# Other figures for DMA transfers in a kernel's own instruction planner

## The chip, the cores and the metric

The kernel runs on one core of one Trainium2 chip. The metric is device time in microseconds, the median of the runs. Work is spread over the engines PE (TensorE, matmuls), DVE (VectorE), ACT (ScalarE), POOL (GpSimd) and SP (SyncE). In this kernel SP does nothing but issue transfers (DMAs), all on one hardware queue.

## The reference

Inputs are x (8 batches, 4224 positions, 192 channels), generator weights (8, 4224, 8 heads, 7 taps), w1 (192 x 768) and w2 (768 x 192); the last two are float64. First a causal dynamic convolution, then an FFT mixing block with a two-layer network:

```python
w = softmax(weight_gen, axis=-1)                 # 7 taps per position and head
x_unf = windows of 7 positions of x_pad          # zeros ahead of the first
x = einsum('bshk,bskhg->bshg', w, x_unf)         # 8 heads of 24 channels
mixed = real(fft(fft(x, axis=1), axis=2))
u = x + mixed
un = (u - mean(u)) / sqrt(var(u) + 1e-6)         # over the 192 channels
out = u + maximum(un @ w_ch1, 0) @ w_ch2
```

## The kernel before, in words

A batch's 4224 positions lie as 128 partitions by 33 rows. Each batch passes through these stages:

- `conv(b)`: loads the generator weights (tile `w`) and x (`x_sb`, in pieces of 192 to 864 KB), makes the softmax on DVE and ACT (`wm`), multiplies rows by taps on DVE (`pr`) and sums them on POOL (`u`). In the first batch some sums run on PE (`pa`). Rows are folded on POOL (`sm`), multiplied by a DFT table on PE (`pg`), put together on DVE (`gt`) and stored to scratch DRAM `g_d`.
- `transform(b)`: loads scratch back as `g` in another layout, multiplies by tables on PE (`pp`) and copies to `pq` on ACT.
- `mix(b, g)`: PE matmuls (`eo`), with sums into `u` on DVE.
- `norm(b, g)`: for one of nine groups of four rows, statistics on ACT (`junk`, `st`, `rs`), normalized rows `un`, split into two float16 parts (`hl`), transposed by DMA into `ht`. For most groups a further DMA copies 64 rows of `ht` to the other partitions as `hd`.
- `mlp(n)`: first products into `ph` on PE, with w1 and the activations as float16 pairs. A part of them uses half of the array's rows: matmuls from `ht` and from `hd` run side by side, alternating. ACT and DVE turn `ph` into the hidden units `hh`; second products go to `po`; DVE adds `po` to `u`, and SP stores `u` to `out`.

None of this is issued as it is written. The functions record operations on a `Tape`. `plan` puts them in order, and `emit` issues each engine's instructions in exactly that order (all at line 408, which is why the profile's rows have that line).

`plan` finds for each operation what it must wait for, then walks all operations as a simulation with one clock for each engine. At each step it takes the earliest moment at which something can start, and of the operations of one engine that can start then, the one of lowest rank. `cost` gives two times for an operation: how long the engine is taken, and how long until the result is there. For transfers it adds a third, the time on the wire. The forward walk keeps one queue for all transfers (`wire`); the backward walk has none. Nine forward rounds at most: the first in the order as written, then up to eight times a backward walk, whose result says how late each operation may start, and two forward walks ranked by that (one of them mixed with the last start times). The plan whose modelled end comes first is kept.

Three rules of the walk matter here. A tile's buffer must be free before its first operation. A group of half-array matmuls is a *visit*: it opens with its first matmul, which reads `ht`, and while it is open PE takes matmuls of that visit alone as long as any of them is waiting. And a transfer occupies SP for 400 ns (1450 for a transpose) in the model, whatever its size.

For a transfer, "run" is the number of elements that lie together on both sides, and the wire time is the number of such runs times a cost per run.

Of the kernel before, what the change touches and what calls it, by code (L numbers as in the profile page):

```python
# [48 lines left out]
POOL_TAPS = {(0, 0): (5, 6), (0, 1): (5, 6), (0, 3): (6,), (1, 0): range(7), (1, 1): range(7)}  # L49
DVE_ADDS = {(1, c): 1 for c in range(2, NC)}  # L50
HOLD3 = 3
WIRE = 0.7

F32_GROUPS = 7
ACT_ROWS = 4
# [121 lines left out]
def together(ap):  # L177

    run = 1
    for step, n in reversed(ap.ap[1:]):  # L180
        if n > 1 and step != run:
            break
        run *= n
    return run
# [7 lines left out]
def cost(op):  # L192

    lane, reads, writes = op.lane, op.reads, op.writes
    count = lambda ap: int(np.prod([n for _, n in ap.ap[1:]]))
    out = writes[0]
    n = max(map(count, reads + writes))
    if lane == "pe":
        n = count(out)
        t = 2 * max(112 if 64 < n <= DH else 56, 0.855 * n) if reads[0].dtype == F32 else max(55.8, 0.417 * n + 2.4)  # L200
        if op.visit:
            return t / 2, t + 178
        return t, t + 178
    if lane == "sp":
        if op.kw.get("transpose"):
            return 1450, 2000 + 1.2 * n, 1.09 * n
        size, run = BYTES[out.dtype], min(together(ap) for ap in reads + writes)
        return 400, 2000 + WIRE * count(out) * size, out.ap[0][1] * count(out) / run * (0.5 + 0.0023 * run * size)
    if lane == "dve":
        t = 150 + (6.27 if op.call == "reciprocal" else 1.042) * n + (60 if len(reads) == 3 and n < 512 else 0)  # L210
        return t - 83, t
    if lane == "pool":
        t = 183 + (1.92 if out.dtype == F16 else 2.13) * n
        return t - 45, t
    t = 190 + (0.833 if out.ap[-1][0] == 1 else 1.666) * n + 90 * (len(reads) - 1)
    return (t + 100, t + 90) if len(writes) > 1 else (t - 95, t)


def plan(tape):
# [29 lines left out]
    for lo, hi, first in tape.holds:  # L249
        for op in ops[lo:min(hi, len(ops))]:  # L250
            if op.lane == first.lane:
                op.needs.setdefault(first.index, False)

    costs = [cost(op) for op in ops]
    before, after = [op.needs for op in ops], [{} for _ in ops]
    for k, needs in enumerate(before):
# [14 lines left out]
    def walk(rank, rows, back=False):  # L271

        to, left = (before, after) if back else (after, before)
        left, ready, span = [len(n) for n in left], [0.0] * len(ops), [None] * len(ops)
        uses = {name: len(set(users[name])) for name in row_of}
        ends, placed, heads = defaultdict(float), {}, {row: 0 for row in rows}
        spare = {row: [(-1e3, i) for i in range(homes[names[0]].bufs)] for row, names in rows.items()}
        free, waiting = {lane: 0.0 for lane in HOP}, {lane: set() for lane in HOP}
        order, table, wire = [], None, 0.0
        half, stays = None, defaultdict(int)  # L280
        taken, wanted = defaultdict(int), {}
        for v in visits:
            stays[v] += 1
        door = set() if back else {span[0] for span in enters.values()}
        for k, n in enumerate(left):
            if n == 0:
                waiting[lanes[k]].add(k)

        def claim(name):

            kind = homes[name].use
            if kind == "fft" and taken["fft"] >= FFT:
                return BANKS
            group = family[name]
            return sum(n for g, n in wanted.items() if g != group)

        def opens(k):

            t = ready[k]
            for name in tiles[k]:  # L300
                if name not in placed:
                    row = row_of[name]
                    if back or row != SHARED:
                        while rows[row][heads[row]] in placed:
                            heads[row] += 1
                        if rows[row][heads[row]] != name:
                            return None
                    if not spare[row] or (row == SHARED and not back and len(spare[row]) <= claim(name)):
                        return None
                    t = max(t, min(spare[row])[0] + HOP[lanes[k]] + (ROOM if row == SHARED else 0))  # L310
            if k in door:
                if len(spare[SHARED]) < 3:
                    return None
                t = max(t, sorted(spare[SHARED])[2][0] + HOP["pe"] + ROOM)
            return t

        for _ in ops:
            at = [(max(free[lane], t), rank[k], k) for lane, ks in waiting.items()
                  for t, k in ((opens(k), k) for k in ks) if t is not None]
            if not at:  # L320
                return None
            if half and stays[half]:
                at = [a for a in at if lanes[a[2]] != "pe" or visits[a[2]] == half] or at
            now = min(at)[0]
            lane = next(lane for lane in HOP if any(t == now and lanes[k] == lane for t, _, k in at))
            k = min((r, k) for t, r, k in at if t == now and lanes[k] == lane)[1]
            if kinds[k] and kinds[k] != table:
                now, table = now + 1283, kinds[k]
            if lane == "pe":
                if visits[k] != half:  # L330
                    now, half = now + VISIT, visits[k]
                stays[half] -= 1
            waiting[lane].remove(k)
            order.append((now, k))
            busy, done, *load = costs[k]
            free[lane], end = now + busy, now + done
            if load and not back:
                wire = max(wire, now + 1000) + load[0]
                end = max(end, wire + 1000)
            span[k] = now, end  # L340
            for name in tiles[k]:
                row = row_of[name]
                if name not in placed:
                    spot = min(spare[row])
                    placed[name] = spot[1]
                    if row == SHARED:
                        taken[homes[name].use] += 1
                        group = family[name]
                        if group in groups:
                            if group not in wanted:  # L350
                                wanted[group] = 6
                            wanted[group] -= 1
                            if not wanted[group]:
                                del wanted[group]
                    spare[row].remove(spot)
                uses[name] -= 1
                ends[name] = max(ends[name], end)
                if not uses[name]:
                    spare[row].append((ends[name], placed[name]))
                    if row == SHARED:  # L360
                        taken[homes[name].use] -= 1
            for j, sync in to[k].items():
                loose = lanes[j] == lane and (lane == "pe" or not sync)
                ready[j] = max(ready[j], now if loose else end + HOP[lane if back else lanes[j]] + (SLACK if lanes[j] != lane else 0))
                left[j] -= 1
                if left[j] == 0:
                    waiting[lanes[j]].add(j)
        return max(end for _, end in span), span, order, placed

    best = now = walk(list(range(len(ops))), rows)  # L370
    for _ in range(TURNED):
        last = {name: max(now[1][k][1] for k in users[name]) for name in row_of}
        turned = walk([-end for _, end in now[1]], {row: sorted(names, key=lambda name: -last[name]) for row, names in rows.items()}, True)
        if turned is None:
            break
        late = [turned[0] - end for _, end in turned[1]]
        now = min((w for w in (walk([part * t + (1 - part) * s for t, (s, _) in zip(late, now[1])], rows) for part in (1.0, 0.8)) if w),
                  key=lambda w: w[0], default=None)
        if now is None:
            break  # L380
        best = min(best, now, key=lambda w: w[0])
# [935 lines left out]
```

## Time and profile before

| | |
|---|---|
| time, median of 3 runs | 1091.94 us (1090.03 to 1092.83) |
| the profiled execution | 1091.01 us |
| its span, first to last instruction | 1089.2 us |
| mean granted TensorE clock | 0.995 |
| PE busy | 1064.2 us, 98% |
| DVE, POOL, ACT busy | 952.3, 871.4, 789.3 us |
| DMA | 130.20 MB, the one queue busy 44.7% of 16 engines |

How to read the rows: a row of waits says who waited for whom, the sum in us, how often, and the longest. A row of the timeline has start, length, engine, line, operation, out<-in, shape and count, and in brackets the idle time before it with what ended it; rows of SP are issues and not transfers. A row of the chain of waits (the work that ended last, followed back) has start and length; where it names a DMA, the length runs from issue until the waiting engine was released. In rows by window each engine has its busy time and, in brackets, its instructions.

### The profile page before, as it was taken

What the parts mean: (1) busy time and instruction counts of PE and PEld (TensorE: products, weight loads), DVE (VectorE), ACT (ScalarE), POOL (GpSimd) and SP (SyncE); (2) the same over time, 40 slices, a digit from 0 to 9 for tenths busy, and PEclk for the clock granted to TensorE, in tenths of its full rate; (3) what the DMA queues carried; (4) which work ended last, traced back from release to release, by engine and by line L of the source; (5) the groups of instructions that cost most, each with busy time, mean ns of one, the idle gap of its engine ahead of it and who ended that gap; (6) DMA issues with size and microseconds to landing.
All of it is one profiled execution on the core that took longest, in us unless ns stands there. A gap on an engine that the chain in (4) does not pass through costs nothing.

```text
span 1089.2 us, 23832 instructions
## 1 busy us (share of the span) xinstructions
PE 1064.2 (98%) x8596; PEld 807.7 (74%) x8596; DVE 952.3 (87%) x1737; ACT 789.3 (72%) x2385; POOL 871.4 (80%) x759
## 2 busy tenths in 40 slices
PE   7899999999999999999999999999999999999998
PEld 5467788886767867687778777687768877786777
DVE  7999998889999998999999999999999998345443
ACT  4575877568874887678886787778786888589842
POOL 4979899799989999799979999799969999102200
PEclk8999999999999999999999999999999999999999
DMA  8554145615484346714564356614554333612311
GB/s 296 158 147 109 31 110 173 157 40 143 101 210 108 83 118 189 153 57 140 129 183 111 98 115 205 146 58 129 147 142 112 79 68 76 147 51 72 90 54 48
DMA packets 166125, 130.20 MB, mean 120 GB/s; under 512 B 119533, under 2 KB 142710, under 8 KB 166006
## 3 DMA queue, kind: packets, MB, share of 16 engines
q1 hardware_dynamic: 166006, 128.67, 44.7%
q8 instruction: 68, 1.11, 0.4%
q14 instruction: 51, 0.42, 0.1%
HBM read 60.38 MB, written 39.43 MB: 92 GB/s over the span
## 4 chain that ended last, share of the span: by engine, by line
PE 54%; DVE 16%; POOL 15%; issue 7%; ACT 4%; DMA 3%; SPq 0%; DVEq 0%; POOLq 0%; ACTq 0%
PE po L408 22%; PE ph L408 22%; POOL u L408 12%; DVE pr L408 5%; PE eo L408 3%; PE pp L408 3%; DVE u L408 3%; DVE wp L408 2%; PE pg L408 2%; PE pa L408 2%; DVE hh L408 2%; ACT junk L408 1%; POOL hl L408 1%; POOL sm L408 1%; DMA g<-g_d 1%
## 5 line engine op out<-in xcount | busy, mean ns | idle before, releaser
L408 POOL TENSOR_TENSOR u<-u,pr 128x768 f32<-128x768 f32 (+1 forms) x396 | 655.9, 1677 | 18.8 <-DVE pr L408 6.9
L408 PE MATMUL po<-w2h,hh 128*128 128x192 f16 x2832 | 423.1, 247 | 1.8 <-DVE hh L408 1.3
L408 PEld LDWEIGHTS <-hh 128*128 128x128 f16 x4248 | 366.1, 99 | 44.2 <-DVE hh L408 1.9
L408 PE MATMUL ph<-ht,w1h 128*128 128x512 f16 (+1 forms) x1296 | 389.7, 362 | 2.1 <-DMA ht<-hl 1.7
L408 DVE TENSOR_TENSOR pr<-x_sb,wp 128x768 f32<-128x768 f32 (+1 forms) x409 | 349.4, 879 | 21.6 <-POOL u L408 17.0
L408 PE MATMUL po<-w2l,hh 128*128 128x192 f16 x1416 | 347.8, 246 | 0.0
L408 ACT ACTIVATE hh<-ph 128x512 f16<-128x512 f32 (+2 forms) x400 | 220.4, 590 | 113.3 <-PE ph L408 82.1
L408 DVE SCALAR_TENSOR_TENSOR hh<-ph,hh 128x512 f16<-128x512 f32 (+1 forms) x358 | 234.1, 680 | 60.1 <-ACT hh L408 59.9
L408 PE MATMUL ph<-ht,w1l 128*128 128x512 f16 (+2 forms) x696 | 230.2, 358 | 0.0
L408 PEld LDWEIGHTS <-w1h 128*128 128x128 f16 x1296 | 127.4, 99 | 109.7 <-issue 25.9
L408 POOL TENSOR_TENSOR hl<-un,hl 128x512 f16<-128x512 f32 (+1 forms) x138 | 116.9, 860 | 73.6 <-issue 40.7
L408 ACT ACTIVATE un<-u,rs 128x192 f32<-128x192 f32 x264 | 126.6, 538 | 23.5 <-POOL rs L408 16.5
L408 ACT ACTIVATE junk<-u,st 128x192 f16<-128x192 f32 x252 | 114.2, 453 | 4.7
L408 ACT ACTIVATE junk<-u 128x192 f16<-128x192 f32 x252 | 91.1, 362 | 28.4 <-DVE u L408 25.1
L408 PEld LDWEIGHTS <-w1l 128*128 128x128 f16 (+1 forms) x864 | 64.1, 97 | 53.5 <-issue 18.0
L408 DVE SCALAR_TENSOR_TENSOR u<-po,isc,u 128x384 f32<-128x384 f32 (+1 forms) x122 | 73.1, 599 | 22.2 <-PE po L408 22.0
L408 PE MATMUL eo<-cs_sb,pq 97*128 97x97 f32 x544 | 88.2, 273 | 0.3 <-ACT pq L408 0.2
L408 PEld LDWEIGHTS eo<-cs_sb,pq 97*128 97x128 f32 x544 | 79.2, 191 | 8.1 <-DVE hh L408 1.2
L408 POOL TENSOR_TENSOR sm<-u 128x382 f32<-128x382 f32 (+1 forms) x128 | 75.7, 608 | 5.8 <-ACT u L408 5.8
L408 ACT COPY pq<-pp 97x204 f32<-97x204 f32 (+3 forms) x176 | 47.2, 314 | 37.4 <-PE pp L408 33.8
L408 PE MATMUL po<-w2f,hh 128*128 128x192 f32 x336 | 74.3, 327 | 0.0
L408 DVE TENSOR_TENSOR u<-u,eo 128x380 f32<-128x380 f32 (+3 forms) x160 | 71.5, 491 | 0.6
(92 smaller groups left out, 1168.8 us busy)
## 6 DMA issues: line engine op xcount, KB each, us to landing
out_dram<-u SPq DMA_DIRECT2D x64, 384.0 KB
x_sb<-in_x_dram SPq DMA_DIRECT2D x48, 384.0 KB
x_sb<-in_x_dram SPq DMA_DIRECT2D x8, 864.0 KB
g<-g_d SPq DMA_DIRECT2D x40, 162.0 KB
g_d<-gt SPq DMA_DIRECT2D x32, 195.0 KB
g_d<-gt SPq DMA_DIRECT2D x32, 189.0 KB
g<-g_d SPq DMA_DIRECT2D x40, 144.0 KB
w<-in_weight_gen_dram SPq DMA_DIRECT2D x6, 924.0 KB
```

The source lines that it names most:

```text
L408: ins = getattr(getattr(nc, op.engine), op.call)(*map(found, op.args), **{n: found(a) for n, a in op.kw.items()}).ins
```

## The change

Only the planner's figures for transfers change; `WIRE` is used in `cost` alone.

```diff
-WIRE = 0.7
+WIRE = 0.5
...
     if lane == "sp":
         if op.kw.get("transpose"):
-            return 1450, 2000 + 1.2 * n, 1.09 * n
+            return 1450, 2000 + 1.2 * n, 1.15 * n
         size, run = BYTES[out.dtype], min(together(ap) for ap in reads + writes)
-        return 400, 2000 + WIRE * count(out) * size, out.ap[0][1] * count(out) / run * (0.5 + 0.0023 * run * size)
+        return 400, 1750 + WIRE * count(out) * size, out.ap[0][1] * count(out) / run * (1.35 + 0.0035 * run * size)
...
             if load and not back:
-                wire = max(wire, now + 1000) + load[0]
-                end = max(end, wire + 1000)
+                wire = max(wire, now + 440) + load[0]
+                end = max(end, wire + 1200)
```

All times are in ns. `count(out)` is the number of elements in one partition, `size` the bytes of one, `out.ap[0][1]` the number of partitions, and `n` the largest count of a transpose's operands (1536 for a full group). The instructions and the transfers are the same before and after; their order on each engine and the buffers that tiles get can differ.

## The prediction

> **What bounds the kernel now.** I read the page's first two parts, then PE's waits, split at 120 us because the picture changes there.
>
> ```profile
> span 1089.2 us, 23832 instructions
> PE 1064.2 (98%) x8596; PEld 807.7 (74%) x8596; DVE 952.3 (87%) x1737; ACT 789.3 (72%) x2385; POOL 871.4 (80%) x759
> PE   7899999999999999999999999999999999999998
> ```
>
> PE is busy 98% of the span, in nearly every slice. The change adds and removes no instruction, so PE's 1064.2 us stay, and what an order of work can win is in the 25.0 us left. Of those, PE waited as follows, first up to 120 us, then from 120 us on.
>
> ```profile
> PE pa L408 <- DVE pr L408: 5.8, 5, 3.6
> PE pg L408 <- POOL sm L408: 2.6, 4, 1.2
> ```
>
> ```profile
> PE ph L408 <- DMA hd<-ht: 2.7, 1, 2.7
> PE ph L408 <- DMA ht<-hl: 1.7, 2, 0.9
> PE po L408 <- DVE hh L408: 1.3, 1, 1.3
> PE ph L408 <- DVE hh L408: 0.5, 1, 0.5
> PE pp L408 <- DMA g<-g_d: 0.7, 1, 0.7
> ```
>
> Up to 120 us PE waits for products and folds, not for transfers. Later transfers are most of it: 2.7 + 1.7 + 0.7 = 5.1 us. Only there can better figures for transfers pay at once. The largest wait also costs clock; the windows show PE's busy time first, then the other engines, then the granted clock before the last two columns.
>
> ```profile
> 384.00:388.00 4.00, 1.37 (x6) 0.39 (x4) 4.00 (x8) 3.48 (x14) 4.00 (x4) 1.00 0.48 174
> 388.00:392.00 4.00, 3.93 (x21) 2.46 (x22) 3.96 (x8) 2.41 (x8) 4.00 (x6) 0.60 0.19 38
> 392.00:396.00 4.00, 4.00 (x31) 2.96 (x29) 2.00 (x5) 2.27 (x7) 4.00 (x4) 0.97 0.39 76
> ```
>
> After the idle 2.70 us the clock is 0.60 for 4 us and 0.97 for 4 more: 4 x 0.40 + 4 x 0.03 = 1.72 us of matmul time. This one wait is thus worth 2.70 + 1.72 = 4.42 us, more than all other transfer waits of PE after 120 us (2.4 us).
>
> **The change, part by part.** Four edits, all in the planner's account of a transfer. Their direct cost on the chip is nothing: what changes is the order on each engine, and which buffer a tile gets.
>
> First, the latency and the bytes (2000 + 0.7 per byte of a partition becomes 1750 + 0.5). For 3072 bytes, a 384 KB load, a store, or a load of g, a lone transfer goes from 4.15 to 3.29 us; the hd copy (1024 bytes) from 2.72 to 2.26 us. Second, queue time (0.5 + 0.0023 per byte of a run becomes 1.35 + 0.0035, times the runs): a 384 KB load takes the queue for 1.55 instead of 0.97 us, an 864 KB load 3.27 instead of 2.10, a hd copy (256 runs of 256 bytes) 0.57 instead of 0.28. Third, the fixed parts around the queue go from 1000 + 1000 to 440 + 1200 ns. Fourth, a transpose holds the queue 1.77 instead of 1.67 us; its own latency is left alone.
>
> So a lone transfer is planned earlier, and one behind others later. The backward walk, which gives the urgencies, has no queue, so it sees only the shorter latencies. Which set is nearer to the chip? The chain of waits has transfers with their true time from issue to release (start, length, what):
>
> ```profile
> 0.74 2.88 DMA w<-in_weight_gen_dram
> ...
> 197.93 3.75 DMA g_d<-gt
> ...
> 202.10 2.93 DMA g<-g_d
> ...
> 340.94 2.65 DMA g<-g_d
> ...
> 684.23 2.88 DMA hd<-ht
> ...
> 808.14 2.87 DMA g_d<-gt
> ...
> 812.30 4.51 DMA g<-g_d
> ```
>
> By the old figures: 3.57, 4.15, 4.15, 4.15, 2.78, 4.15, 4.15; by the new: 2.99, 3.29, 3.29, 3.29, 3.30, 3.29, 3.7 (the last behind three loads of g). The old miss by 0.79 us on average, the new by 0.46. The transfer that PE stood still for, with what SP issued just ahead of it and the sizes of those:
>
> ```profile
> 379.70 0.85 SPq L408 DMA_DIRECT2D out_dram<-u  x1
> 380.61 1.16 SPq L408 DMA_DIRECT2D x_sb<-in_x_dram  x2
> 381.87 0.62 SPq L408 DMA_DIRECT2D hd<-ht  x1
> ```
>
> ```profile
> x_sb<-in_x_dram SPq DMA_DIRECT2D x1, 864.0 KB
> x_sb<-in_x_dram SPq DMA_DIRECT2D x1, 384.0 KB
> out_dram<-u SPq DMA_DIRECT2D x1, 96.0 KB
> ```
>
> ```profile
> 381.87 6.16 DMA hd<-ht
> ```
>
> ```profile
> 384.98 0.39 PE L408 MATMUL ph<-ht,w1l 64*128 64x512 f16 x1
> 388.07 0.39 PE L408 MATMUL ph<-hd,w1l 64*128 64x512 f16 x1 [2.70 <-DMA hd<-ht]
> ```
>
> Replayed with the true issue times, taking the 864 KB first. Old: the store ends on the queue at 380.99, the big load at 381.61 + 2.10 = 383.71, the next at 384.68, the copy at 384.96, seen at 385.96. New: the store at 380.66, then 381.05 + 3.27 = 384.32, 385.87, 386.44, seen at 387.64. In truth 388.02. The old figures hide 2.1 us of this delay from the planner, the new ones 0.4. An order that looked almost free (PE reaches the visit at 384.98, about 1 us early by the old account) now looks 2.7 us dear. I therefore take it that the plan chosen from the walks avoids it: -4.42 us. Both ends: 0 if the order there stays, and -4.42 - 2.4 = -6.8 if the ht and g waits go as well. I take -4.42 because a transpose's own latency is not touched, so nothing points at the ht waits.
>
> [...]
>
> **What is late next.** Where the plan moves the copy ahead of the x loads, these land 0.57 us later by the new account. Who waits for them is the next batch's products on DVE and the sums on POOL. Both are full at that place (4.00 of 4 us above), so they have a backlog to work through, and this costs 0 while it lasts. If that cover is gone, it costs the 0.57 us, once for each batch: 4.0 us over 7 batches. Where the plan lets PE do other products first, the copy's hidden units on ACT and DVE move later by the same 2.7 us, and the second products of that group behind them; PE has the previous group's second products as cover.
>
> **The sum.** The profiled execution took 1091.01 us, 1.8 us more than its span of 1089.2. 1091.01 - 4.42 = 1086.6 us. The median of the three runs, 1091.94, is 0.93 us higher, so for a median I add that: 1087.5 us.
>
> **The rivals.** (a) *Nothing of weight changes.* The walk is greedy: it lets PE enter a visit of half products when ht is there, whatever it knows of hd, and then stays. Knowing the true landing does not by itself stop it, and about 1 us of this wait was accepted already. The stall then stays or comes up elsewhere at the same price: 1091.9 us, with 1088.7 to 1095.2 as what can't be told from no change (0.3% of 1091.94 is 3.3 us). For it: the edits move planned times by about 1 us where PE's backlog covers most. Against it: 497 transfers move, and the walk sorts exact times, so one changed landing can reorder all that follows it.
>
> (b) *The other side: more visits entered before their copy lands.* The list of issues counts the copies:
>
> ```profile
> hd<-ht SPq DMA_DIRECT2D x56, 64.0 KB
> ```
>
> PE stalls at one of the 56. A lone copy is planned 0.46 us sooner, so visits are entered sooner; a copy that falls behind one 864 KB load then costs 4.42 us as priced above. With the stall kept and one more: 1091.9 + 4.4 = 1096.4; two more: 1100.8. It decides from the first net extra stall, since 4.4 is over 3.3. For it: the chosen entry does not look at hd. Against: wherever something big is queued ahead the new figures are later, not sooner.
>
> (c) *The queue times are too long where the queue is really full.* Over the first 20 us, in 40 slices of 0.5 us:
>
> ```profile
> GB/s 0 0 0 40 139 394 377 419 430 151 34 194 373 221 387 359 387 334 450 392 395 430 410 418 365 410 416 406 406 399 399 412 393 399 393 395 407 390 395 398
> DMA packets 2453, 6.56 MB, mean 328 GB/s; under 512 B 253, under 2 KB 765, under 8 KB 2453
> ```
>
> The chip moves about 400 GB/s from 10 us on. The old figure for a 384 KB load is 393216 / 0.97 = 406 GB/s, the new 254. So at the start the old figures are right, and the new plan thinks the later x, table and weight loads arrive up to some 9 us later than they do (6.56 MB at 254 instead of 400 GB/s). If it puts the second half of the softmax on DVE behind products that are not needed yet, the taps after it come later by that block:
>
> ```profile
> 12.34 1.50 DVE L408 TENSOR_REDUCE wm<-w 128x184 f32<-128x1288 f32 x1
> ...
> 14.00 1.49 DVE L408 TENSOR_TENSOR w<-w,wm 128x1288 f32<-128x1288 f32 x1
> ...
> 18.91 1.50 DVE L408 TENSOR_REDUCE wm<-w 128x184 f32<-128x1288 f32 x1
> ...
> 21.70 1.31 DVE L408 RECIPROCAL wm<-wm 128x184 f32<-128x184 f32 x1
> ```
>
> That is 5.8 us, giving 1091.9 + 5.8 = 1097.7, and it decides from 3.3 us, a little more than half of the block. Against it: between 13 and 60 us no row of the engines' waits names a transfer, so the loads have slack, and by the new account this piece (644 KB) is planned for 12.9 us, close to where it is used.
> [...] The trace is on both sides: 400 GB/s here, and a copy at 388.02 that only the longer queue time explains.
>
> **How the numbers follow.** The stall gone, nothing like it new: 0.42, at 1087.5, own range 1083 to 1088.7. It includes 1085.1, where the ht and g waits go too. (a) 0.25. (b) 0.20, since a new order of 23832 instructions finds new places as easily as it loses old ones. (c) 0.10. The rest, 0.03, is a start that gets worse in another way. So faster 0.42, within 0.3% 0.25, slower 0.33. The range of 8 in 10 takes in one and two extra stalls above, and below the 1085.1 and some of PE's 8.4 us of waits up to 120 us: 1081 to 1101.
>
> **What would show it.** PE's wait for hd gone or under 1 us and the granted clock at 1.00 between 360 and 420 us; PE busy still about 1064 us; the 384 and 864 KB loads no longer just ahead of a copy that a visit waits for. PE's first product of the hidden layer is this row:
>
> ```profile
> 104.01 0.38 PE L408 MATMUL ph<-ht,w1h 128*128 128x512 f16 x1 [0.31 <-DVE bn L408]
> ```
>
> Wrong, if there are waits of PE for hd at two or more places (b), or if that first product comes over 3 us later than 104 us (c). If PE's waits for DVE hh grow instead, the loss is of a kind that I have not priced.

## The result, and the profile after

The changed kernel took 1098.08 us, median of five runs (1095.53 to 1100.12), against 1091.94 before: a ratio of 1.0058, 95% interval 1.0037 to 1.008. It is slower, by about 6 us (0.6%); the forecast was 4.4 us faster. The profiled execution is the 1100.12 us one, 9.1 us over the profiled execution of before. The first page of the changed kernel, span and busy time of each engine, then PE in 40 slices of 27 us:

```profile
span 1098.3 us, 23862 instructions
PE 1065.1 (97%) x8596; PEld 807.9 (74%) x8596; DVE 961.5 (88%) x1737; ACT 786.7 (72%) x2385; POOL 871.5 (79%) x759
PE   7899997999999999999999999999999999999998
```

PE's work is the same (1065.1 against 1064.2 us). Two things are new: slice 7 of PE (165 to 192 us) has fallen from 9 to 7, and DVE, with the same 1737 instructions, is busy 9.2 us longer. PE's waits from 120 us on:

```profile
PE mr_w L408 <- DVE mx_w L408: 7.4, 1, 7.4
PE po L408 <- DVE hh L408: 4.2, 6, 1.8
PE pp L408 <- DMA g<-g_d: 3.7, 4, 1.2
PE ph L408 <- DMA ht<-hl: 1.0, 1, 1.0
```

The row for `hd<-ht` (2.7 us before) is gone, as forecast, and the loads have moved away from the copy, as forecast too: before, SP issued that copy 1.3 us after the 864 KB load and 0.4 us after the 384 KB one (starts 380.61, 381.43 and 381.87 us); the same copy, the tenth, now goes out 6.6 and 2.5 us after them (388.35, 392.47 and 394.94). In its place are longer waits for `hh` (1.3 before) and `g` (0.7 before), and one that no row of before has: 7.4 us for DVE's `mx_w`. The place in the timelines of DVE, POOL and PE (start, length, engine, line, operation):

```profile
177.50 0.94 DVE L408 TENSOR_TENSOR pr<-x_sb,wp 128x768 f32<-128x768 f32 x1
178.36 8.89 DVE L408 TENSOR_SCALAR mx_w<-mx_w 128x3 int32<-128x3 int32 x1
187.29 0.16 DVE L408 TENSOR_REDUCE mx_w<-mx_w 128x1 f32<-128x3 int32 x1
```

```profile
177.44 8.83 POOL L408 TENSOR_TENSOR u<-u,pr 128x768 f32<-128x768 f32 x5
186.24 0.98 POOL L408 TENSOR_TENSOR sm<-u 128x382 f32<-128x382 f32 x1
189.35 1.81 POOL L408 TENSOR_TENSOR u<-u,pr 128x768 f32<-128x768 f32 x1 [2.12 <-DVE pr L408]
```

```profile
187.50 0.79 PE L408 MATMUL mr_w<-ident,mx_w 128*128 128x128 f32 x2 [7.42 <-DVE mx_w L408]
```

The DVE row at 178.36 masks three columns, the exponents of w2's maxima, in the scale of w2 (`weight_scale`). In before it is this row:

```profile
169.28 0.31 DVE L408 TENSOR_SCALAR mx_w<-mx_w 128x3 int32<-128x3 int32 x1
```

So the same instruction takes 8.89 us instead of 0.31. It ends at 187.25, when POOL has run six instructions back to back (the last ends at 187.22) and pauses, because its supplier DVE stands still. The windows of the changed kernel around the new wait, and one around the place of the old `hd` wait (PE's busy time first; the granted clock before the last two columns):

```profile
182.00:186.00 4.00, 0.00 (x0) 0.00 (x0) 4.00 (x1) 0.00 (x0) 4.00 (x3) 0.65 0.00 0
186.00:190.00 4.00, 2.50 (x8) 1.97 (x9) 3.96 (x12) 0.00 (x0) 1.88 (x3) 0.50 0.24 55
190.00:194.00 4.00, 4.00 (x14) 2.90 (x13) 4.00 (x11) 3.62 (x7) 3.13 (x3) 0.57 0.93 288
388.00:392.00 4.00, 4.00 (x28) 1.91 (x26) 3.79 (x9) 3.90 (x17) 4.00 (x5) 1.00 0.66 178
```

At 388 us the clock is 1.00 where it was 0.60. Behind the new wait 2.50 us ran at 0.50 and 4.00 us at 0.57, that is 1.25 + 1.72 us of matmul time. With 7.42 us of idling it makes 10.4 us. The store of `out` serves as a milestone; here is the third store, the fifth, and the last two, first of before, then of the changed kernel:

```profile
166.10 0.37 SPq L408 DMA_DIRECT2D out_dram<-u  x1
198.49 0.37 SPq L408 DMA_DIRECT2D out_dram<-u  x1
1085.37 1.62 SPq L408 DMA_DIRECT2D out_dram<-u  x2
```

```profile
164.12 0.37 SPq L408 DMA_DIRECT2D out_dram<-u  x1
206.84 0.35 SPq L408 DMA_DIRECT2D out_dram<-u  x1
1094.50 1.62 SPq L408 DMA_DIRECT2D out_dram<-u  x2
```

The changed kernel is 2.0 us ahead at the third store, 8.4 us behind at the fifth and 9.1 behind at the end. Between the third and the fifth it loses 10.3 us, which is more than the whole loss, and the 10.4 us of that one wait account for it. Behind the fifth store it loses another 0.8 us, although the `hd` wait of 2.7 us is gone there.

### The profile page after: what moved, and what is told of

The parts are those of the page before. It is cut to its first block, busy times and chain, and to the rows that moved or that the text cites. A ratio compares the mean times of both kernels' runs of the same rounds, so it can differ in the third digit from the quotient of the medians.

```text
span 1098.3 us, 23862 instructions
## 1 busy us (share of the span) xinstructions
PE 1065.1 (97%) x8596; PEld 807.9 (74%) x8596; DVE 961.5 (88%) x1737; ACT 786.7 (72%) x2385; POOL 871.5 (79%) x759
## 4 chain that ended last, share of the span: by engine, by line
PE 43%; DVE 20%; POOL 19%; issue 12%; DMA 4%; ACT 2%; SPq 1%; POOLq 0%; DVEq 0%
PE po L408 18%; PE ph L408 17%; POOL u L408 15%; DVE pr L408 6%; DVE u L408 3%; DVE hh L408 3%; POOL hl L408 3%; PE eo L408 2%; PE pp L408 2%; DVE wp L408 2%; POOL sm L408 1%; PE pg L408 1%; DMA x_sb<-in_x_dram 1%; DVE mx_w L408 1%; DMA g<-g_d 1%
## 5 line engine op out<-in xcount | busy, mean ns | idle before, releaser
L408 PE MATMUL po<-w2h,hh 128*128 128x192 f16 x2832 | 416.6, 246 | 5.2 <-DVE hh L408 4.2
L408 PE MATMUL po<-w2f,hh 128*128 128x192 f32 x336 | 76.9, 333 | 0.0
L408 PEld LDWEIGHTS po<-w2f,hh 128*128 128x128 f32 x336 | 61.8, 194 | 13.1 <-issue 0.7
```

What stands on the lines that cost most here:

```text
L408: ins = getattr(getattr(nc, op.engine), op.call)(*map(found, op.args), **{n: found(a) for n, a in op.kw.items()}).ins
```

## The experiments

**Is it the mask, and its form?** The order of the changed kernel, with the mask issued as three single columns:

```diff
-        nc.vector.tensor_scalar(out=ex, in0=mx[:, 0:n].bitcast(I32), scalar1=mask, ...)
+        # emitted, for w2, as one instruction for each column j
+        nc.vector.tensor_scalar(out=ex[:, j:j + 1], in0=mx[:, j:j + 1].bitcast(I32), scalar1=mask, ...)
```

> The changed kernel's plan, instruction for instruction, but the one DVE instruction that took 8.89 us there (the exponent mask of w2's scale, 128x3 int32) is issued as three of 128x1. Theory A (that instruction was shut out by POOL's sums, which ran back to back beside it; the 128x1 instructions beside busy POOL took 0.15 us): it takes under 1 us in all, PE's 7.4 us wait for it and the half clock after it go, the 10.6 us lost around 185 us come back: 1098.1 - 10.6 = 1087.5, between 1085 and 1090. Rival B (the new order has DVE late there anyway, and the long instruction is only where it shows): the wait moves to the next instruction, 1095 to 1100. Rival C (any mask beside POOL is shut out): three long instructions, over 1100.

Measured: 1092.26 us, ratio to before 1.0016 (1.0004 to 1.0027), span 1090.5, so 7.8 us less in the profiled executions. DVE's timeline:

```profile
178.47 0.27 DVE L412 TENSOR_SCALAR mx_w<-mx_w 128x1 int32<-128x1 int32 x3
182.91 6.26 DVE L412 TENSOR_TENSOR isc<-sc_w,sc_w 128x1 f32<-128x1 f32 x1
```

At the same place beside the same POOL run, three single columns take 0.27 us in all, and PE's wait for `mx_w` is gone. But the next small instruction with two input tensors, `isc` (0.33 us in before), is now the one that stands: 6.26 us beside POOL's back-to-back instructions. PE waits 3.2 us for `w2l` behind it, and the order's lead of 2.7 us at the fourth store (184 us in before) becomes 2.9 us behind at the fifth. The time lies in none of the three ranges: the mask's form was the cause of its stand, as A said, but another instruction took its place.

**Is the mask slow wherever POOL is busy?** The kernel before, with the mask moved later, to just ahead of its reader, into a run of POOL sums:

```diff
+    moved = order.pop(step_of)            # w2's mask
+    order.insert(<place of the reduction that reads it>, moved)
     emit(real, tc, ctx, nc, order, placed)
```

> The kernel before, with its own plan, but the same mask instruction is moved 16 places down DVE's order, to just ahead of the reduction that reads it. There POOL has a row of sums ready (13.05 us of eight without a gap). Theory A: it is shut out until POOL runs out of ready sums, 4 to 9 us; PE reaches the matmul that waits for it 3.8 us later, so PE loses 1 to 5 us and perhaps 1.7 us of clock: 1093 to 1099. Rival B (place does not matter, only the new order): 0.15 to 0.3 us as before, 1091 to 1093.

Measured: 1090.12 us, ratio 1.0 (0.999 to 1.001). A miss: the mask took only 0.42 us in the middle of three sums on POOL.

```profile
176.86 0.42 DVE L408 TENSOR_SCALAR mx_w<-mx_w 128x3 int32<-128x3 int32 x1
```

```profile
175.41 5.41 POOL L408 TENSOR_TENSOR u<-u,pr 128x768 f32<-128x768 f32 x3
```

It got in when the running sum ended. A busy POOL alone thus does not make the stand last over several POOL instructions.

**Does the split itself change anything?** The kernel before with the same split, again of w2's mask alone:

```diff
-        nc.vector.tensor_scalar(out=ex, in0=mx[:, 0:n].bitcast(I32), scalar1=mask, ...)
+        nc.vector.tensor_scalar(out=ex[:, j:j + 1], in0=mx[:, j:j + 1].bitcast(I32), scalar1=mask, ...)
```

> The kernel before, with its own plan, the mask issued as three 128x1 instructions at its old place. It took 0.31 us there, so both theories: no change, 1090 to 1093. A control for the kernels that have the split.

Measured: 1091.54 us, ratio 1.0004 (0.999 to 1.0019); the `hd` wait stays at 2.6 us. The form alone is worth nothing where the instruction is not held. This run also shows something about the wait itself. Its clock behind the wait is the last figure but two of these windows:

```profile
390.05 0.39 PE L412 MATMUL ph<-hd,w1l 64*128 64x512 f16 x1 [2.56 <-DMA hd<-ht]
```

```profile
388.00:392.00 4.00, 1.95 (x15) 1.06 (x16) 4.00 (x7) 3.48 (x14) 4.00 (x4) 1.00 0.02 3
392.00:396.00 4.00, 4.00 (x34) 3.08 (x32) 3.65 (x8) 2.46 (x9) 4.00 (x5) 1.00 0.51 98
```

The same wait in the same order cost no clock here. In the kernel with the mask moved it was 2.71 us long, and the next 4 us ran at 0.57. So the 1.72 us of clock that the prediction counts with this wait come and go with the execution.

**The figures' own effect.** The changed kernel's order with the mask split, and `isc` written with one input tensor and a column as its scalar:

```diff
-        nc.vector.tensor_tensor(out=isc, in0=scales[0][:, 1:2], in1=s2[:, 1:2], op=ALU.mult)
+        nc.vector.tensor_scalar(out=isc, in0=scales[0][:, 1:2], scalar1=s2[:, 1:2], scalar2=None, op0=ALU.mult)
```

> The order of after, instruction for instruction, with two DVE instructions of the 188 us region issued in another form: w2's mask as three of 128x1, and isc as a 128x1 TENSOR_SCALAR whose scalar is a column, so that it has one input tensor in place of two. Theory (the whole loss lies in DVE instructions shut out by POOL's run of instructions, and the figures' own effect is the predicted gain): with only the mask cured the ratio was 1.0016, its span 1090.5, and isc stood shut out for 6.26 us, during which the difference of the stores grew by 5.6 us; with both cured that goes too, so 1084 to 1088 us against about 1091 to 1092 before, a ratio of 0.994 to 0.997, and no DVE instruction of 128x1 above 1 us between 170 and 200 us. Rival (what is gained at the start and at 385 us is given back all along the kernel whatever happens at 188 us): the difference of the stores still wanders back to about zero and the ratio stays within 0.003 of 1. Rival (a third instruction takes the place of isc): a row of over 3 us of a small DVE instruction appears, and the ratio stays at 1.000 to 1.003.

Measured: 1087.71 us (1086.5 to 1089.71), ratio 0.9962 (0.9948 to 0.9976): faster than both kernels, and in the range that the theory gave. `isc`, the stores, and PE's waits after 120 us:

```profile
181.90 0.21 DVE L412 TENSOR_SCALAR isc<-sc_w,sc_w 128x1 f32<-128x1 f32 x1
```

```profile
163.22 0.36 SPq L412 DMA_DIRECT2D out_dram<-u  x1
195.85 0.34 SPq L412 DMA_DIRECT2D out_dram<-u  x1
1082.01 1.62 SPq L412 DMA_DIRECT2D out_dram<-u  x2
```

```profile
PE po L412 <- DVE hh L412: 4.2, 6, 1.8
PE pp L412 <- DMA g<-g_d: 2.2, 2, 1.6
```

No third instruction took the place. But the stores also bear out a part of the first rival: this kernel is 2.9 us ahead at the third store, 2.6 at the fifth, 3.4 at the end. The lead comes from the start; from the third store on, the order wins 0.5 us net although the `hd` wait is gone. Even that is not more than executions differ: from the third store to the last but one, four executions of before's order (before itself, with its mask split, with its mask moved, and the kernel with the transposes' figure changed, below) took 917.9 to 920.1 us, and this kernel 918.8. One loss is the order's: PE's waits for `hh` at `po` are 4.2, 3.5 and 4.2 us in the three profiles of the changed order and 1.3 in each of those four. The wait for `g` is not: it is 2.2 us here, and 0.2 to 2.8 in those four.

**Which forms does POOL hold?** The kernel before with extra DVE instructions on a small tile that nothing reads any more, in two sets:

```diff
+            if FIRST <= done < LAST and (done - FIRST) % EVERY == 0:    # EVERY = 40, then 25
+                # one small instruction, its form by turns
```

> The order of before, with 26 extra DVE instructions on a small tile that nothing reads any more, one after each 40th DVE instruction, in three forms: TENSOR_SCALAR 128x3 int32 (the mask's form), TENSOR_TENSOR 128x1 with two tensor inputs (isc's form), TENSOR_SCALAR 128x1. It measures the shut-out by itself. Theory: the first two forms start only where POOL lets them: beside an idle POOL 0.1 to 0.4 us, beside a busy one until the end of its running instruction or of several, so up to 2 us and in some places 4 to 9 us; the 128x1 TENSOR_SCALAR takes 0.1 to 0.3 us wherever it stands. Rival (the mask and isc were long for another reason than POOL, such as their inputs being written just before): no probe is over 0.5 us. Rival (any DVE instruction can be shut out): the 128x1 TENSOR_SCALAR is as long as the others. The time is some 0.5 to 30 us above before, by how many of the probes are long.

> The order of before with 42 extra DVE instructions on a small tile that nothing reads any more, one after each 25th DVE instruction, in five forms: TENSOR_SCALAR 128x2 int32, a copy of 128x1, a copy of 128x3, TENSOR_REDUCE 128x3 to 128x1, SCALAR_TENSOR_TENSOR 128x1. It tells which forms POOL shuts out; the runs so far show it for TENSOR_SCALAR 128x3 (median 0.96 to 1.6 us, longest 6.07) and TENSOR_TENSOR 128x1 with two tensors (longest 7.19), and not for TENSOR_SCALAR 128x1 (0.14 to 0.15, five of five). [...] Rival (it is the mask's and isc's own operations): the copies are all short. Rival (any small instruction but the single TENSOR_SCALAR): the reduction is long too.

Measured: 1119.44 and 1127.0 us, one execution each. Of the first set, grouped by form (busy us and mean ns behind the bar):

```profile
L426 DVE TENSOR_SCALAR mx_w<-mx_w 128x3 int32<-128x3 int32 x11 | 27.4, 2493 | 0.0
L422 DVE TENSOR_TENSOR mx_w<-mx_w 128x1 f32<-128x1 f32 x10 | 12.5, 1253 | 0.0
L426 DVE TENSOR_SCALAR mx_w<-mx_w 128x1 int32<-128x1 int32 x5 | 0.7, 145 | 0.0
```

Of the second set, from the view of the tile (shortest, median and longest in ns):

```profile
L423 DVE TENSOR_SCALAR mx_w<-mx_w x9: 177/887/5259, 238.0 to 864.9; 128x2 int32<-128x2 int32 x9
L426 DVE COPY mx_w<-mx_w x9: 146/149/154, 257.5 to 880.9; 128x1 f32<-128x1 f32 x9
L428 DVE COPY mx_w<-mx_w x8: 161/848/6337, 271.7 to 819.6; 128x3 f32<-128x3 f32 x8
L430 DVE TENSOR_REDUCE mx_w<-mx_w x8: 148/150/158, 286.1 to 830.9; 128x1 f32<-128x3 f32 x8
L432 DVE SCALAR_TENSOR_TENSOR mx_w<-mx_w x8: 149/724/5833, 298.5 to 847.0; 128x1 f32<-128x1 f32 x8
```

One of the long ones, with POOL's row beside it:

```profile
362.83 6.07 DVE L426 TENSOR_SCALAR mx_w<-mx_w 128x3 int32<-128x3 int32 x1
```

```profile
360.00 8.89 POOL L413 TENSOR_TENSOR u<-u,pr 128x768 f32<-128x768 f32 x5
```

POOL's row ends at 368.89, DVE's at 368.90. Held are scalar operations on two or three columns, a copy of three, and both forms with two input tensors (the longest of each form 5.26 to 7.19 us); never the single-column scalar operation and copy, nor the reduction (22 of these, 0.14 to 0.16 us; 19 of them beside a running POOL instruction). All three rivals on form fall. Of the 46 instructions of held forms, 35 took up to 1.65 us, at most one POOL sum (1.8 us), and 11 took 4.5 to 7.2 us, over three to five POOL instructions; none lies between. Of the 11, 9 got in only when POOL paused for 0.25 us or more.

**The four figures, one at a time.** First the queue times alone, with the mask split; then, with mask and `isc` in the free forms, the latencies alone, the transposes alone, the fixed times alone, and all but the latencies.

```diff
-... * (0.5 + 0.0023 * run * size)
+... * (1.35 + 0.0035 * run * size)
```

> Of the figures, only the queue time by rows and bytes is changed (1.35 + 0.0035 for 0.5 + 0.0023), with the mask split so that POOL cannot shut it out. Theory D (the longer queue time is what lets the planner see the late hd copy): PE's wait for hd at 385 us is gone, about 1087.5, 1084 to 1091. Rival E (a new order is a draw, and the hd wait goes or stays by chance): anywhere from 1084 to 1098, with waits at other places.

```diff
-WIRE = 0.7
+WIRE = 0.5
-        return 400, 2000 + WIRE * count(out) * size, ...
+        return 400, 1750 + WIRE * count(out) * size, ...
```

> The kernel before with the latency figures alone changed (the fixed part 2000 to 1750, WIRE 0.7 to 0.5), and the two DVE instructions in the forms that POOL does not shut out. Theory (a new order is a draw: each has waits of its own at places that no figure of transfers governs): between 1086 and 1097 us, ratio 0.995 to 1.005, with the hd wait at 385 us still there, since the queue times are the old ones. Rival (the latency figures carry the change): as after with both instructions cured, 1084 to 1088.

```diff
-            return 1450, 2000 + 1.2 * n, 1.09 * n
+            return 1450, 2000 + 1.2 * n, 1.15 * n
```

> The kernel before with the queue time of the DMA transposes alone changed (1.09 to 1.15 per column), and the two DVE instructions in the forms that POOL does not shut out. This edit says next to nothing new of the machine, so it shows what any change of the order is worth. Theory (a draw): within 0.5% of before, either side, with its own set of PE waits of 1 to 5 us at places other than before's. Rival (only edits of weight move the time): the ratio is 1.000 within 0.001 and PE's waits are those of before.

```diff
-                wire = max(wire, now + 1000) + load[0]
-                end = max(end, wire + 1000)
+                wire = max(wire, now + 440) + load[0]
+                end = max(end, wire + 1200)
```

> The kernel before with the two fixed times alone changed (1000 to 440 ns ahead of a transfer, 1000 to 1200 ns behind it), and the two DVE instructions in the forms that POOL does not shut out. Theory (the hd wait goes with the queue times alone): the hd wait stays at 2 to 3 us, ratio 0.998 to 1.002. Rival (the fixed times carry the gain): hd wait gone, 0.996.

```diff
 # the changed kernel, with these two lines as before
-WIRE = 0.5
+WIRE = 0.7
-        return 400, 1750 + WIRE * count(out) * size, ...
+        return 400, 2000 + WIRE * count(out) * size, ...
```

> After without its latency edit (the queue times, the fixed times and the transposes changed), with the two DVE instructions in the forms that POOL does not shut out. Theory (the hd wait goes with the queue times, and the start's 1.5 to 3 us with the latency figures, which the run with these alone had: its first store was 2.6 us ahead): hd wait gone, first store within 1 us of before, ratio 0.996 to 1.000. Rival (the gain of after with both cured is the queue times' alone): 0.996. Rival (each order is a draw): PE waits for DVE's hh and for g of 3 to 8 us, ratio 1.000 to 1.003, as for the queue times alone.

| figures changed | us | ratio to before, interval | PE's wait for `hd` |
|---|---|---|---|
| queue times | 1092.71 | 1.001 (0.9994 to 1.0026) | none |
| latencies | 1091.4 | 1.0007 (0.999 to 1.0024) | 0.3 us |
| transposes | 1090.87 | 0.998 (0.9962 to 0.9999) | 2.2 us |
| fixed times | 1090.11 | 0.9996 (0.9976 to 1.0016) | none |
| all but latencies | 1088.9 | 0.9987 (0.9971 to 1.0002) | 0.2 us |
| all (the figures' own effect, above) | 1087.71 | 0.9962 (0.9948 to 0.9976) | none |

With the latencies alone the `hd` wait was expected to stay; it went, but for 0.3 us. It went with the fixed times alone too, where it was also expected to stay. With the queue times alone it went as expected, but the time missed its range of 1084 to 1091 us. With all but the latencies the first store was expected within 1 us of before's and came 2.0 us ahead.

The transposes' figure changes next to nothing in the order: POOL, ACT and SP have before's order, on PE one `po` product moves, by up to ten places, at three spots, and DVE differs by the free forms alone. This run is thus before's order with both free forms, and it shows what executions and these forms make: PE's wait for `hd` stays (2.2 us), while that for `g` is 2.8 us instead of 0.7 and that for `ht` 2.6 instead of 1.7. Its ratio of 0.998 lies just outside the 0.001 that the rival allowed. Set beside this run instead of before, the changed order with both free forms is 3.2 us faster (1087.71 against 1090.87, ten executions each, 1086.5 to 1089.71 and 1088.59 to 1094.42), or 0.3%. PE's largest waits after 120 us, with the queue times alone, and then with the fixed times alone:

```profile
PE ph L412 <- DVE hh L412: 3.0, 5, 1.5
PE pp L412 <- DMA g<-g_d: 2.6, 3, 1.8
PE ph L412 <- DVE u L412: 2.1, 3, 0.9
```

```profile
PE ph L412 <- DMA ht<-hl: 2.5, 3, 1.6
PE ph L412 <- ACT hh L412: 2.3, 1, 2.3
```

Each order has waits of its own, 1 to 3 us each. All of PE's waits from 120 us on add up to 8.2 us with all figures and 9.9 with the latencies alone; the four executions of before's order have 7.7 to 10.0, so one profile of each does not rank the orders by this sum. The theory of a draw gave 0.995 to 1.005 for the latencies; the three figures that change the order when taken alone (queue times, latencies, fixed times) give 0.9996 to 1.001, the two runs with several figures 0.9987 and 0.9962. Which figure brings the 0.4% of all together can't be told from these intervals.

## Why the prediction was wrong

The step that failed is the sum: its only term was -4.42 us, and it had none for an instruction that takes longer in its new place. "What is late next" priced late transfers and late hidden units. Nothing in it asked whether a DVE instruction's length depends on what POOL does beside it. That missing term measured 10.4 us in the profile (7.42 us of idling, 2.97 of clock), and with both held instructions in free forms the same plan loses it: 1087.71 us, where 1087.5 was forecast.

That these two numbers meet is luck for the most part: of the 3.4 us between the two profiles 2.9 come from the start, which the sum left out, and 0.5 from all behind the third store. Step by step:

- *The `hd` wait goes*: right; no row, the loads no longer go out just ahead of the copy, and the clock is 1.00 from 360 to 420 us. The reason given, that the longer queue time shows the planner the delay, is not shown: the wait also went with only the latencies or only the fixed times changed. All five orders that differ much from before's lost it, or all but 0.3 us of it.
- *-4.42 us for it*: too much. Its 1.72 us of clock are not always lost: the same wait was followed by a clock of 1.00 in the kernel with the split. And in the plan with free forms 2.9 us of `hh` waits came instead, a loss that the prediction named and had not priced. The stores show 0.5 us net from the third on, which is within what executions differ by.
- *Up to 120 us nothing*: the start was faster, and not in the sum. PE's first product of the hidden layer came at 101.54 us instead of 104.01. A part of this lies in the execution: with the same order, kernel before and the split of it, the window before 120 us reads

```profile
80.00:120.00 40.00, 37.72 (x280) 29.99 (x279) 35.77 (x97) 24.98 (x67) 40.00 (x26) 1.00 0.30 78
```

```profile
80.00:120.00 40.00, 37.98 (x263) 29.08 (x262) 33.24 (x93) 23.01 (x62) 39.51 (x26) 0.91 0.30 78
```

  with a clock of 1.00 and 0.91. Set against before's profile, the third store lies between 1.9 us ahead and 2.2 behind in five executions of before's order up to there (2.6 behind in the kernel with the transposes' figure), and 1.9 to 2.9 ahead in the three of the changed order. The means of the five and the three differ by 2.1 us, which is likely the order's, with few executions to say it.
- *The rivals*: (b) gave 1096.4 us, near the result, but by copies that land after their visit is entered; there was none. (c) gave a late start; it was early. The side of the result was covered, its cause was not.

The profile of before held the hint. Its mask of w2 takes 0.31 us beside a running POOL instruction, and the same mask of w1, with POOL idle, takes 0.17:

```profile
70.03 0.17 DVE L408 TENSOR_SCALAR mx_w<-mx_w 128x3 int32<-128x3 int32 x1
```

The stand of an instruction is not bounded by one POOL instruction: the changed kernel's mask stood beside six, none over 1.8 us. DVE's main work, `pr`, has two input tensors as well and is not held: in before its 361 instructions of 128x768 took 0.92 to 0.97 us, 355 of them beside a running POOL instruction. One of its inputs, `wp`, lies in PSUM, while the inputs of the held instructions all lie in SBUF; no run changed the place of an input alone. What holds an instruction is not shown. The runs show which forms are held, and that some of them end with POOL's run (the mask at 187.25 with 187.22, a probe at 368.90 with 368.89).

Why some win the first gap between two POOL instructions and others lose three to six in a row stays open. The kernel with the mask moved shows that POOL being busy does not decide it, and no experiment told what does.

## What to carry to other kernels

When an order changes, look for the small DVE instructions that stand on PE's path (masks, scales, maxima) and ask what POOL runs beside them: a form with two input tensors, both in SBUF here, or a copy or scalar operation on two or three columns, at times took 4.5 to 8.9 us there, while the same work by single columns took 0.27 us for three, and a two-tensor product rewritten with a column as its scalar took 0.21. A stall that a planner's new figure removes is not yet a gain: a new order brings waits of its own, and here the gain from the removed one did not show in the stores behind it. It also pays to profile the old order more than once: its waits for two transfers differed by 1 to 3 us from one execution to the next. And a sum that meets the measured time should be checked at milestones along the kernel, since it may be met by other terms than its own.

## What the hardware showed that was not expected

An instruction of three elements on each partition took 8.89 us beside POOL, 60 times the 0.15 us of its single-column form. The held small instructions took either up to 1.8 us (1.65 in the probes, 1.81 for `isc` in the changed kernel) or 4.5 to 8.9 us, with nothing between. The granted clock between 80 and 120 us was 1.00 in one execution and 0.91 in another of the same order. And an idle time of PE of 2.56 us was followed by a clock of 1.00, one of 2.22 us (the transposes' run) by 0.57 over 4 us.
